# An S4 convolution block with a GEGLU: four early buffers, a small transfer scratch and a re-drawn order of tasks

## The chip, the cores and the metric

The kernel runs on one core of a Trainium2 chip. The core has a matrix engine (TensorE, PE in the profile), a vector engine (VectorE, DVE), an activation engine (ScalarE, ACT), GpSimd (POOL) and SyncE (SP). Each runs its own list of instructions in order, and they meet at semaphores. SP issues most transfers between memory and the on-chip SBUF. ACT and POOL issue a few of them. The metric is the device time of one launch in microseconds. Before the change it is 782.71 us, the median of three runs that lie between 780.6 and 785.24.

## The reference

One sequence of L = 2048 rows with D = 448 channels is taken through two halves of a block. Six rows of 448 numbers, made from the conditioning vector `c`, scale, shift and gate the halves.

```python
mod = (silu(c) @ w_mod).reshape(1, 6, 1, -1)
sa, ca, ga, sb, cb, gb = (mod[:, i] for i in range(6))
h = layernorm(x) * (1 + ca) + sa
x = x + ga * s4(h)
h = layernorm(x) * (1 + cb) + sb
x = x + gb * ((gelu(h @ w_gate) * (h @ w_up)) @ w_down)

def s4(u):
    dt = exp(log_dt)
    K = Re( sum_n C[d,n] * exp(dt * A[d,n] * l) * dt * B[d,n] )   # l = 0..L-1, 256 n per d
    return irfft(rfft(u, 2L) * rfft(K, 2L))[:L] + u * Dskip
```

The gate and up weights are 448 x 1792 each, the down weight is 1792 x 448. All inputs and the output are 32-bit floats.

## The kernel before, in words

**Tasks and their order.** The kernel doesn't call its engines where it describes the work. Each step is a task: `add(name, engine, ...)` records a name, an engine (or a choice of engines), a closure that emits the instructions, and the tasks it depends on. `Plan.order` then sorts all tasks by one number each and emits them in that order. The number comes from the table `PLACE`: for each name, a list of positions, one for each task of that name in the order of creation. A letter behind a number picks the engine where there is a choice (a for ACT, d for DVE, p for POOL, s for SP). Every engine executes its own tasks in that order. So the table sets which transfer stands ahead of which in a queue, and which copy stands ahead of which product on DVE. A wait on one task holds up everything behind it on the same engine.

**Three stages.** The work falls into three parts, and the table puts them one behind the other with overlaps.

1. *The filter and its spectrum.* The 448 channels are handled in subsets of 8, and these in three groups (the third one smaller). Four calls of `prep` load and prepare A, B, C and dt (`p.*`; the load `p.ld` at two loads a call), and `lt0`, `lt1` load prepared rows back. For each subset PE forms exponents and angles (`x.mm`, `y.mm`, `ang`, `anc`, lines 657 to 675). ACT takes exponentials (`x.exp`, `y.exp`, L644, L662), and sines and cosines (`sin`, `cos`, `sin2`, `cos2`, L680 to L699; `mag` at L683 strips a sign on DVE or ACT). DVE forms two products (`tx` at L721, `tyc` at L725). PE sums over n (`kgen`, L748). `kev` copies the sums out of PSUM. `kd`, `ka` and `kout` (L771 and after) do the first step of the transform of K, and leave it in `ako`. Beside this, the rows of x are loaded (`x.ld`, L852), normalized (`bn` at L877, `norm`) and taken through the first step of their own transform (`as`, `ua`, L984), which goes by memory (`ua.st` to u_d, `ub.u` back as ui, `ub.st` to us_d). The conditioning rows are made on the way (`m.ld`, `m.mm`). For groups 0 and 1, `k_fft` then works in batches. `f.fc` loads a piece of the constant matrices, and `f.ut` loads the spectrum of x. `f.fwd` (L1094) transforms K, `f.pr` (L1098) multiplies the spectra on DVE, `f.inv` (L1105) transforms back, `f.z` copies the result out of PSUM (by the helper at L482, ACT or DVE), and `f.st` (L1113) stores it to memory as y.
2. *The third group and the turn of the layout.* `ev_end` (task `ev.end`, L1051) closes the SBUF pools of the filter stage and opens those of the rest. `t_fft` does the spectra of the third group in nine pieces: `t.fwd`, `t.p0` and `t.p1` (products on DVE), `t.i0` with the copy `t.z0` and the store `t.s0` (L1224, to yb_d) for the rows that the first block of the output needs, and later `t.inv`, `t.z`, `t.st` (L1231) for the others. `yi.e` (L1288) loads what the first block needs of groups 0 and 1 (four transfers, all of them waiting for the stores of y), and `yi.l0`, `yi.l1` (L1297) load back from yb_d what the third group gives, piece by piece, by SP, ACT or POOL. `x1.ld` (L1265) loads the 512 rows of x of a block. The last step of the inverse transform for the first block is `co.mme` (L1404, channels of groups 0 and 1, 320 of them) and `co.mml` (L1409, the other 128). `co.adde` and `co.addl` (L1415, L1416) add x and take statistics on DVE. `co.rt` to `co.cb` normalize, scale and turn the result. The first weight tiles arrive by `w.le` (SP) and `w.la`, `w.ld` (all at L1332). Each is split in a high and a low half-precision part, `w.hi` (L1345, ACT) and `w.lo` (L1349 and L1350, DVE). A few idle matmuls (`spin`) and one idle square root on ACT (`warm`) stand where nothing else is to be done.
3. *The GEGLU.* There are four blocks of 512 rows. PE forms gate and up (`gu2`, `gu`, L1524, L1530), ACT the gelu (L1537), DVE the product (L1544). ACT and DVE split it again (L1556, L1559). PE does the down projection (L1599, L1630). The remaining `co.*` tasks of blocks 1 to 3 are worked in between, with `yi.ld` (L1278) and `x1.ld` for each.

**Where the early data lives.** Four loads of stage two have no input that depends on earlier work: the 896 KB of x rows for block 0 (`x1.ld` number 0), the first weight tile of 512 KB (`w.le` number 0), and two constants of 32 KB, `c.ai` (the matrix of `co.mm`) and `c.ih` (an identity in half precision, used by `spin` and the turns). In the kernel before, their buffers belong to pools that `ev_end` opens (`yp`, `ws`), so the four loads depend on `ev.end`. The weight loads depend on the x load `t_x` as well.

Of the kernel before, what the change touches and what calls it, by code (L numbers as in the profile page):

```python
# [11 lines left out]
FT = mybir.dt.float32  # L12
HF = mybir.dt.float16
# [10 lines left out]
L, D, N, FF = 2048, 448, 256, 1792  # L24
# [387 lines left out]
def s4_geglu(ctx: ExitStack, tc: tile.TileContext, a: dict, out: bass.AP):  # L412
    nc = tc.nc
# [1420 lines left out]
```

## Time and profile before

| | us |
|---|---|
| three runs | 780.6, 782.71, 785.24 |
| the profiled execution, its own time | 783.97 |
| its span | 782.0 |
| PE busy in the span | 728.2 |
| DVE busy | 590.7 |
| ACT busy | 459.6 |
| POOL busy | 8.4 |

The profile is one execution taken by the hardware profiler. Its mean granted TensorE clock is 0.993 of full speed. The span is the stretch from the first to the last instruction in the records, and 1.97 us of the device time lie outside it. A row of a group says: line, engine, operation, output <- inputs, shapes, count, then the busy time and the mean in ns of one, then the idle time of the engine just before these instructions, and what ended most of it. A row of a timeline says: start, length, engine, line, operation, output <- inputs, count, and in brackets the idle time just before and the event that ended it. Names with q behind an engine (SPq, DVEq) are the engine's own sequencer, which issues transfers. Engines overlap, so busy times don't add up to the span.

### The profile page before, as it was taken

How to read it: one execution, taken by the hardware profiler on the slowest of the kernel's cores; microseconds unless marked ns; L12 is line 12 of the kernel's file. 1: busy time of each engine (PE TensorE's matmuls, PEld its weight loads, DVE VectorE, ACT ScalarE, POOL GpSimd, SP SyncE). 2: the span in 40 equal slices, each digit the busy share in tenths (PEclk: the TensorE clock that was granted, in tenths of full speed). 3: DMA queues.
4: the chain of work that ended last, by engine and by line, in shares of the span. 5: the costliest groups of instructions: out<-in, count | busy, mean ns of one | idle time of the engine just before them, and what ended most of it. 6: DMA issues, size and time to landing. Idle time of an engine off the chain costs nothing.

```text
span 782.0 us, 19039 instructions
## 1 busy us (share of the span) xinstructions
PE 728.2 (93%) x8166; PEld 443.6 (57%) x8166; DVE 590.7 (76%) x889; ACT 459.6 (59%) x615; POOL 8.4 (1%) x23
## 2 busy tenths in 40 slices
PE   3677889998899999989999999999999999999998
PEld 1234444444577777677774445444694446944477
DVE  6999999999899999979767952569774587034743
ACT  5899998999899999862554730233411334022330
POOL 0000000000000000001200000000000000000000
PEclk9999999999999999999999999999999999999999
DMA  8645569998887598888876884355337224013201
GB/s 264 190 140 177 143 159 273 254 300 248 210 237 243 161 258 244 238 303 238 253 234 227 281 217 132 130 177 168 140 66 224 95 95 135 14 48 98 79 2 60
DMA packets 103950, 139.87 MB, mean 179 GB/s; under 512 B 34388, under 2 KB 85492, under 8 KB 103866
## 3 DMA queue, kind: packets, MB, share of 16 engines
q1 hardware_dynamic: 100436, 132.53, 57.8%
q10 hardware_dynamic: 2950, 5.38, 2.1%
q8 instruction: 64, 1.05, 0.6%
q0 software_dynamic: 480, 0.75, 0.3%
q14 instruction: 20, 0.16, 0.1%
HBM read 100.39 MB, written 36.01 MB: 174 GB/s over the span
## 4 chain that ended last, share of the span: by engine, by line
PE 66%; ACT 9%; DMA 8%; DVE 7%; issue 3%; SPq 2%; ACTq 0%; POOL 0%; DVEq 0%; POOLq 0%
PE pq L1530 24%; PE pq L1630 9%; PE pf L1105 5%; PE pg L675 4%; PE kg L748 4%; PE pd L1599 4%; PE pf L1094 3%; PE kg L771 2%; DMA w<-in_wgu 2%; PE pq L1524 2%; PE pd L1630 2%; ACT fg L688 1%; ACT my L662 1%; PE pf L984 1%; DVE ty L725 1%
## 5 line engine op out<-in xcount | busy, mean ns | idle before, releaser
L1530 PE MATMUL pq<-ht,wr 128*128 128x512 f16 (+1 forms) x1200 | 248.5, 365 | 0.4 <-DMA ht<-hl 0.4
L1530 PEld LDWEIGHTS <-wr 128*128 128x128 f16 x1200 | 114.5, 98 | 128.5 <-issue 11.8
L725 DVE TENSOR_TENSOR ty<-my,fg 128x2048 f32<-128x2048 f32 x56 | 127.6, 2281 | 0.0
L1537 ACT ACTIVATE ge<-pq 128x512 f32<-128x512 f32 (+1 forms) x60 | 33.8, 565 | 102.1 <-PE pq L1524 64.3
L1544 DVE TENSOR_TENSOR fq<-ge,pq 128x512 f32<-128x512 f32 (+1 forms) x60 | 38.9, 649 | 72.3 <-PE pq L1530 44.3
L1556 ACT ACTIVATE hh<-fq 128x1024 f16<-128x1024 f32 (+1 forms) x49 | 46.7, 961 | 65.0 <-DVE fq L1544 46.4
L721 DVE TENSOR_TENSOR tx<-mx,fg 128x1024 f32<-128x1024 f32 x56 | 67.8, 1216 | 4.4 <-ACT fg L692 3.0
L1630 PE MATMUL pq<-d,hh 128*128 128x224 f16 x476 | 68.9, 259 | 0.0
L748 PEld LDWEIGHTS kg<-ty,tx 128*32 128x32 f32 x3584 | 52.8, 110 | 21.6 <-issue 13.4
L748 PE MATMUL kg<-ty,tx 128*32 128x64 f32 x3584 | 61.5, 220 | 3.5 <-issue 1.6
L1559 DVE TENSOR_TENSOR hlo<-fq,hh 128x1024 f16<-128x1024 f32 (+1 forms) x49 | 53.7, 1106 | 13.4 <-ACT hh L1556 13.3
L1630 PE MATMUL pq<-d,hlo 128*128 128x224 f16 x238 | 61.7, 259 | 0.0
L688 ACT ACTIVATE fg<-pg 128x1024 f32<-128x1024 f32 x56 | 57.8, 1037 | 2.1 <-DVE tx L721 2.0
L662 ACT ACTIVATE my<-pg 128x1024 f32<-128x1024 f32 x56 | 55.5, 1033 | 3.7 <-PE pg L657 3.1
L1630 PEld LDWEIGHTS <-hh 128*128 128x128 f16 x560 | 54.2, 98 | 0.9 <-issue 0.2
L1105 PE MATMUL pf<-q,fc 128*128 128x160 f32 x264 | 43.4, 314 | 1.0 <-DVE q L1098 0.7
L1105 PEld LDWEIGHTS pf<-q,fc 128*128 128x128 f32 x264 | 37.5, 194 | 7.8 <-issue 4.7
L692 ACT ACTIVATE fg<-fg,small 128x1024 f32<-128x1024 f32 x36 | 41.4, 1170 | 0.1
L675 PEld LDWEIGHTS <-lt 64*128 64x128 bf16 x304 | 18.0, 94 | 37.1 <-issue 24.0
L675 PE MATMUL pg<-ea,lt 64*128 64x512 bf16 x152 | 31.4, 388 | 6.9 <-ACT fg L688 2.1
L1747 ACT ACTIVATE d<-fq 128x896 f16<-128x896 f32 x14 | 13.3, 947 | 39.8 <-PE pd L1599 27.3
L680 ACT ACTIVATE fg<-pg 128x1024 f32<-128x1024 f32 x30 | 31.1, 1037 | 2.0 <-PE pg L675 1.7
(208 smaller groups left out, 1121.8 us busy)
## 6 DMA issues: line engine op xcount, KB each, us to landing
wr<-w_d SPq DMA_DIRECT2D x21, 896.0 KB
fc<-in_k_fc SPq DMA_DIRECT2D x20, 576.0 KB
u_d<-so SPq DMA_DIRECT2D x32, 224.0 KB
ui<-u_d SPq DMA_DIRECT2D x10, 672.0 KB
fq<-in_wd SPq DMA_DIRECT2D x14, 448.0 KB
w<-in_wgu SPq DMA_DIRECT2D x11, 512.0 KB
us<-uo SPq DMA_DIRECT2D x22, 240.0 KB
q<-us SPq DMA_DIRECT2D x22, 240.0 KB
```

The source lines that it names most:

```text
L662: A.activation(yb.tile.rearrange("p h (n k) -> p n h k", n=2), pb.tile.rearrange("p (n h k) -> p n h k", n=2, h=2), AF.Exp)
L675: T.matmul(pa[:, nh * 512:nh * 512 + 512], w, x, start=(k == 0), stop=(k == 2))
L688: A.activation(fb.tile[:, 0].rearrange("p x (n k) -> p n x k", n=2), pb.tile.rearrange("p (n x k) -> p n x k", n=2, x=2), AF.Sin, scale=TW ...
L692: A.activation(fb.tile[:, 1], fb.tile[:, 1], AF.Sin, scale=-TWO_PI, bias=halfpi)
L721: V.tensor_mul(tx.tile, xb.tile[:, xm, None, :].to_broadcast([128, 2, 512]), fb.tile[:, :, 0])
L725: V.tensor_mul(ty.tile, yb.tile[:, :, None, :].to_broadcast([128, 2, 2, 512]), fb.tile[:, None, :, 1].to_broadcast([128, 2, 2, 512]))
L748: T.matmul(kg[32 * g:32 * g + 32, 2 * (s % 2) + q, :64], tx[:, r, nh, 4 * q + g], ty[:, 0:4:3, nh, 4 * q + g] if r else ty[:, 1:3, nh, 4 * ...
L1105: T.matmul(pz.tile[:, e % 32 - sl0], fc.tile[:, i, 1 + t], pp.tile[:, t, i], start=(t == 0 and e != 32), stop=(t == 1 and e != 0))
L1530: T.matmul(pb.tile[k][:, ts], wr.tile[:, 4 * lo + t, k, c0:c0 + 128], ht[:, m, ts], start=f % 2 == 0 and i == 0, stop=f % 2 == 1 and i == 9)
L1556: A.activation(hg.tile[0][:, cb, c], fq.tile[:, c], AF.Copy)
L1559: V.tensor_sub(hg.tile[1][:, cb, c], fq.tile[:, c], hg.tile[0][:, cb, c])
L1630: T.matmul(bank(k)[:, m], x[:, p, q[0], ts], w[:, p, q[1]], start=new and m == 0 and p == 0 and z == 0, skip_group_check=True, stop=i in ( ...
```

## The change

A new pool `ahead` is opened at the start of the kernel and stays to its end. It holds the two constants, the x rows of blocks 0 and 2, and the first weight tile. Those four loads lose their dependence on `ev.end` (and on `t_x`). The size of the scratch for dynamic transfers is given as 2048 bytes. Nothing else in the code differs but the table.

```diff
     keep = ctx.enter_context(tc.tile_pool(name="keep", bufs=1))
+    ahead = ctx.enter_context(tc.tile_pool(name="ahead", bufs=1, reuse_waits="tile"))
...
-        K2["ai"] = POOLS["yp"].tile([128, 64], FT, name="ai", bufs=1)
-        K2["ih"] = POOLS["yp"].tile([128, 128], HF, name="idenh", bufs=1)
...
-    K2 = {}
+    K2 = {"ai": ahead.tile([128, 64], FT, name="ai"), "ih": ahead.tile([128, 128], HF, name="idenh")}
...
-            xb.tile = POOLS["wk" if blk % 2 else "yp"].tile([128, 4, D], FT, name="x1", bufs=1)
+            xb.tile = (POOLS["wk"] if blk % 2 else ahead).tile([128, 4, D], FT, name="x1", bufs=1)
...
+        zero = cb + k == 0
...
-            wb.tile = POOLS["ws"].tile([128, 4, 256], FT, name="w")
+            wb.tile = (ahead if zero else POOLS["ws"]).tile([128, 4, 256], FT, name="w")
...
-            t1 = add("w.le", {"SP": 0.42}, -1350 + k + 2 * cb, ld, [EV["end"], t_x], [wb], kb=540)
+            t1 = add("w.le", {"SP": 0.42}, -1350 + k + 2 * cb, ld, [] if zero else [EV["end"], t_x], [wb], kb=540)
...
-    c_ai = sp("c.ai", 58, lambda: K2["ai"], lambda: a["k_ai"], 32, [EV["end"]])
-    c_ih = sp("c.ih", 58, lambda: K2["ih"], lambda: a["k_ih"], 32, [EV["end"]])
-    t_x = x1_load(0, [EV["end"]])
+    c_ai = sp("c.ai", 58, lambda: K2["ai"], lambda: a["k_ai"], 32)
+    c_ih = sp("c.ih", 58, lambda: K2["ih"], lambda: a["k_ih"], 32)
+    t_x = x1_load(0, [])
...
-    nc = _bacc.Bacc("TRN2", target_bir_lowering=False, num_devices=1)
+    nc = _bacc.Bacc("TRN2", target_bir_lowering=False, num_devices=1, dynamic_dma_scratch_size=2048)
```

In `PLACE` nearly every position below about 1480 is different, and nearly all from 1481 on are the same. The rows that the steps of this text touch, each with its positions before and after (long rows are cut behind the first entries):

```diff
-    "c.ai": "1250",
+    "c.ai": "133",
-    "c.ih": "1254",
+    "c.ih": "516",
-    "x1.ld": "1269 1463 1661 1782",
+    "x1.ld": "286 1463 1661 1782",
-    "w.le": "1304 1290 1351",
+    "w.le": "196 1300 1323",
-    "x.ld": "33 4 226 156",
+    "x.ld": "19 10 214 139",
-    "p.ld": "0 7 86 87 170 265 368 452",
+    "p.ld": "0 3 83 84 201 260 314 475",
-    "m.ld": "27 36 17 433 558 761",
+    "m.ld": "29 31 30 420 578 760",
-    "ub.u": "386 431 443 468 509 534 564 596 608 637 667",
+    "ub.u": "421 431 454 486 528 537 550 601 643 657 664",
-    "lt0": "61 112 302 369 561 744 852 1017",
+    "lt0": "64 144 325 368 560 801 861 985",
-    "lt1": "95 162 384 432 742 745 965 1060",
+    "lt1": "92 195 326 369 723 802 968 986",
-    "f.fc": "726 746 779 808
+    "f.fc": "724 731 767 790
-    "f.fwd": "727 759 786 809
+    "f.fwd": "746 759 787 820
-    "f.z": "755a 772d 812d 832a 865a 887d 908d 928a
+    "f.z": "757a 781a 809a 835a 869a 895d 912a 920a
-    "kev": "218d 224a 290d 317a 373d 394d 448a 490a
+    "kev": "199d 230d 290a 345a 378d 393a 462a 518d
-    "warm": "1263",
+    "warm": "1377",
-    "spin": "1353 1387 1388 1389 1392 1412",
+    "spin": "1394 1395 1396 1412 1413 1416",
-    "yi.l0": "1369s 1360s 1335p 1367p 1345s 1337p 1354p 1371p 1368p",
+    "yi.l0": "1309s 1344s 1342p 1315p 1353s 1347p 1351p 1357p 1359p",
-    "w.hi": "1341 1343 1356 1421 1460 1468 1487
+    "w.hi": "1267 1372 1363 1426 1455 1477 1487
```

312 rows, old and new, of the table PLACE are left out of this document.

## The prediction

> **What bounds the kernel now.** I read the windows view first, cut at the three points where the work changes its kind: the start, the last copy of the third group's K (349 us), the first gate/up matmul (387.4 us). Columns are span, then busy time and instructions of PE, PE weight loads, DVE, ACT, POOL, then clock, DMA share and GB/s.
>
> ```profile
> 0.00:349.00 349.00, 302.45 (x5294) 187.57 (x5294) 328.20 (x419) 318.66 (x403) 0.87 (x10) 0.99 0.78 224
> 349.00:387.40 38.40, 35.65 (x391) 29.88 (x392) 31.38 (x61) 14.91 (x32) 6.82 (x12) 1.00 0.81 245
> 387.40:782.00 394.60, 390.11 (x2484) 226.15 (x2482) 231.15 (x409) 125.98 (x182) 0.69 (x1) 1.00 0.44 133
> ```
>
> Stage one (0 to 349) belongs to DVE, with ACT 9.5 us behind it: DVE idles 20.8 us in all. Stage three belongs to PE: 390.11 of 394.60. Its time hardly depends on the order, and nearly all positions from 1481 on are the same in the new list. So a change of the total is a change of the moment at which stage three starts, now 387.4. Between them lies a short second stage, where a chain of small transfers decides. The chain of waits, in order of time:
>
> ```profile
> 360.03 4.92 DMA yb_d<-z
> ...
> 370.38 4.67 DMA yi<-yb_d
> ...
> 378.86 0.43 PE pd L1409 x4
> ...
> 387.45 2.29 PE pq L1530 x20
> ```
>
> Results of the last group go to memory (yb_d), come back turned (yi), and only then do the matmuls at L1409 (co.mml) run, at 378.86. Why the first yb_d store starts as late as 360.03 is seen on SP's queue. The first answer is of 340 to 360, the second of 356 to 360:
>
> ```profile
> 348.20 0.43 SPq L1265 DMA_DIRECT2D x<-in_A_u  x1
> 348.72 0.38 SPq L1113 DMA_DIRECT2D y<-zo  x1
> 349.20 10.73 SPq L1288 DMA_DIRECT2D yi<-y  x4
> 360.03 0.54 SPq L1224 DMA_DIRECT2D yb_d<-z  x1
> ```
>
> ```profile
> 358.71 1.22 SPq L1288 DMA_DIRECT2D yi<-y  x2
> ```
>
> The last two yi<-y issues wait for the y<-zo store of 348.72, and that store was issued right behind the 896 KB of x rows (348.20). SP stands until 358.71, and the yb_d stores stand behind it. POOL, which fetches most of yi back, waits for those stores and then has a backlog of seven issues:
>
> ```profile
> 369.29 3.81 POOL L1297 DMA_DIRECT2D yi<-yb_d  x7 [2.94 <-DMA yb_d<-z]
> ```
>
> **The change part by part.** The profiled run took 783.97 us: a span of 782.0 and 1.97 around it. It is 1.26 above the median of the runs shown, 782.71. The terms below are differences, so I apply them to the median as well.
>
> *The early buffers (x1.ld 1269 to 286, w.le[0] 1304 to 196, c.ai 1250 to 133, c.ih 1254 to 516).* No work is added. SP issues the same four transfers, of 896, 512, 32 and 32 KB. At the old place x rows leave the queue ahead of the y store: 0.918 MB at the 245 GB/s of 349 to 387 is 3.7 us. So SP should come free near 355 to 357 rather than 358.7 to 360, about when the first results (z0) exist. What then ends last in stage two is DVE. Its rows:
>
> ```profile
> 368.23 0.49 DVE L1415 TENSOR_TENSOR x<-x,pd 128x320 f32<-128x320 f32 x1
> 368.75 0.49 DVE L1416 BATCH_NORM_STATS2 st<-x 128x6 f32<-128x320 f32 x1
> ...
> 370.65 0.96 DVE L1349 SCALAR_TENSOR_TENSOR wr<-w,wr 128x768 f16<-128x768 f32 x1 [0.49 <-ACT wr L1345]
> 371.62 0.42 DVE L1350 SCALAR_TENSOR_TENSOR wr<-w,wr 64x256 f16<-64x256 f32 x1
> ...
> 377.05 0.96 DVE L1349 SCALAR_TENSOR_TENSOR wr<-w,wr 128x768 f16<-128x768 f32 x1 [1.87 <-ACT wr L1345]
> ...
> 379.33 0.29 DVE L1415 TENSOR_TENSOR x<-x,pd 128x128 f32<-128x128 f32 x1 [0.88 <-PE pd L1409]
> ```
>
> The spectral products end at 368.2; their number and place are the same in the new list. From there to the first addl (L1415 on 128 columns, 379.33) DVE has four adde of about 1.0 (0.49 and 0.49) and three w.lo of 1.4 (0.96 and 0.42). The new list adds one z0 copy, which waits for its matmuls, and one t.z copy. I estimate 0.9 and 0.7 for the two from the rows around them, which all last 0.4 to 1.0. Sum: 368.2 + 4.0 + 4.2 + 1.6 = 378.0, against 379.33, with no wait left in it: -1.3. The waits it replaces are the 1.87 and the 0.88, so the gain lies between 0 and 2.75. At worst the yb_d round trip still ends at 378.86 and nothing is gained. The new order also sends yi loads of finished pieces earlier on POOL (1315 against 1335) and lets the warm-up square-root table load go into ACT's wait (1377). I take **-1.6** for the stage, near the DVE sum and inside 0 to -2.75.
>
> *The new order in stage one: the start.* First tx on DVE waits for ACT:
>
> ```profile
> 42.30 1.23 DVE L721 TENSOR_TENSOR tx<-mx,fg 128x1024 f32<-128x1024 f32 x1 [0.95 <-ACT fg L699]
> ```
>
> Four sine passes stand ahead of it now, three in the new list (cos2 of the second subset goes behind), one pass of about 1.0 less. **-0.95**, between 0 (the wait comes elsewhere) and -0.95. Loads are re-sorted, but the five large ones ahead of the first K work stay the same bytes.
>
> *The first FFT batch.* PE waits for the filter constants, then DVE waits for PE:
>
> ```profile
> 199.00 1.46 PE L1094 MATMUL pf<-ako,fc 128*128 128x160 f32 x6 [1.86 <-DMA fc<-in_k_fc]
> ```
>
> ```profile
> 204.23 1.22 DVE L683 TENSOR_SCALAR fg<-pg 128x1024 int32<-128x1024 int32 x1 [2.36 <-PE pg L675]
> ```
>
> Today f.fc[0] stands at 726 and f.fwd[0] directly behind at 727, and six loads of lt follow in the same queue (742 to 745). In the new list the load is at 724 and its matmuls at 746, with six PE tasks between; two of the three lt pairs come later (801, 802), the third stands one place ahead of it. Bounds 0 and -2.36; I take half, **-1.2**, as one lt load is still in front.
>
> *Moves between ACT and DVE.* The list counts: f.z five fewer on DVE, kev two more, mag one more, ub.ev, p.e0, p.c0 (two) and so on. The two large prices:
>
> ```profile
> L683 DVE TENSOR_SCALAR fg<-pg 128x1024 int32<-128x1024 int32 x6 | 7.3, 1218 | 2.5 <-PE pg L675 2.4
> ...
> L482 DVE COPY zo<-pf 128x480 f32<-128x480 f32 x10 | 6.5, 649 | 0.2
> ...
> L482 DVE COPY ke<-kg 128x252 f32<-128x252 f32 x14 | 5.7, 410 | 0.8 <-PE kg L748 0.7
> ```
>
> -5 x 0.649 + 2 x 0.41 + 1.218 = -1.2 on DVE, and about -0.8 for the small ones: -2.0, and about as much more on ACT, which has 9.5 us more idle time but is as full in the middle. Between 0 and -2.0; I take half, **-1.0**.
>
> *What may cost.* In the new list m.ld[3] (784 KB) stands ahead of ub.u[0], whose matmuls follow three places later; today it stands behind. At 195 GB/s (row below) that is 0 to +4.1; SP can issue it while it still waits for the u_d stores, so I take 0. The early x and w loads run under stage one; 0 is taken, and their bound is the second rival. ACT's functions follow one another in the new list with as many changes of table as today: 0.
>
> *Sum:* -1.6 - 0.95 - 1.2 - 1.0 = -4.75. From the profiled run 779.2; from the median **778.0**.
>
> *Small scratch (2048 bytes).* Rows of POOL's transfers, by tile and by issue (KB each, us to landing):
>
> ```profile
> L1297 POOL DMA_DIRECT2D yi<-yb_d x10: 543/547/702, 365.7 to 374.2; - x10
> ```
>
> ```profile
> yi<-yb_d POOLq DMA_DIRECT2D x9, 32.0 KB, 4.5
> ```
>
> An issue takes 0.55 us, a landing 4.5: POOL does not wait for one to land before it issues the next. I take 0; the upper end is the third rival. The Trainium skill, "SBUF — State Buffer" (section "SBUF size: 192, 224, or 256?"), says that this scratch, 16 KiB by default, holds the ring of descriptors that POOL writes for its transfers. The Trainium skill, "DMA: Bandwidth & Descriptors" (section "Terms"), gives 16 bytes to a descriptor, by which, as an estimate, 2048 bytes hold 128 for each engine; no run here shows the limit. The Trainium skill, "SBUF — State Buffer" (section "SBUF: two separate sides"), speaks against the change's many POOL issues under a busy DVE: it has such a transfer take about 3.1 us instead of 0.62, and ten of them would add 25 us. By that rule the time would be that of the third rival; the trace does not agree, since the issues at 365.7 and after took 0.55 to 0.70 beside a DVE that worked without a gap.
>
> **The rivals.**
>
> 1. *Given back.* SP's gain is real but stage one finds new waits of the size of the old ones. Rows for: every wait named above is under 3 us and hangs on the order, and one that no order explains stays:
>
> ```profile
> 333.17 1.23 DVE L721 TENSOR_TENSOR tx<-mx,fg 128x1024 f32<-128x1024 f32 x1 [2.51 <-ACT fg L692]
> ```
>
> Two waits like this (2 x 2.4) cancel the sum: 782.71, say 780.5 to 784.5.
>
> 2. *The early loads collide (slower).* The w load (512 KB) and p.ld[4] (448 KB) are placed ahead of x.ld[2]. Today:
>
> ```profile
> 64.92 0.35 SPq L852 DMA_DIRECT2D xt<-in_A_u  x1
> ```
>
> ```profile
> 70.49 0.62 DVE L877 BATCH_NORM_STATS2 st<-xt 128x6 f32<-128x448 f32 x1
> ```
>
> ```profile
> 60.00:70.00 10.00, 7.05 (x112) 3.25 (x101) 9.76 (x13) 9.94 (x13) 0.00 (x0) 1.00 0.64 195
> ```
>
> From issue to first use are 5.57 us, of which 0.918 MB at 195 GB/s take 4.7: 0.9 of slack. 0.98 MB ahead cost 5.0, so DVE, which works in order, would stand 4.1 at the statistics with all its tx and ty behind them. The x rows (4.7 more) stand ahead of the puts of prep(1) and of lt0[2]. Sum +8.8: 786.8. It decides if the w load is still under way when x.ld[2] is issued. Against: the DMA share there is 0.64, and the w load waits for nothing, so SP can issue it early.
>
> 3. *POOL becomes serial* (ring too small, or the port rule): ten loads at 4.5 to landing, from about 364 (365.7 today, less the 1.6), end at 409 instead of 378.86: +30, 813.
>
> 4. *All waits go:* -2.75 - 0.95 - 2.36 - 2.0 - 2.51 = -10.6: 772.1.
>
> **How the numbers follow.** Forecast (775.5 to 780.5) 0.42; rival 1 0.23; rival 2 0.19; rival 3 0.03; rival 4 0.13. About 0.5% (3.9 us) is what a measurement of this kernel can tell from no change: below 778.8 is faster, above 786.6 slower. Faster: two thirds of the forecast (0.27) and rival 4: 0.40. Same: the rest (0.15) and rival 1: 0.38. Slower: rivals 2 and 3: 0.22. The range goes from rival 4's 772 to just above rival 2's 786.8, leaving out rival 3 and the worse half of rival 2.
>
> **What would show it.** Right: no x<-in_A_u on SP near 348; the second yi<-y pair under 356; first addl near 378; the first L1530 near 382 to 384 when the terms of stage one are in it. The fc wait at the first L1094 is short. Wrong: DVE waits before L877 near 70 us, or PE before the first L984 (rival 2); POOL issues of L1297 over 1 us or in steps of 4 (rival 3); a stage three longer than 394.6, which would mean that the order of the weights, not the start, has become the limit.

## The result, and the profile after

The changed kernel takes 777.02 us, the median of seven runs between 775.92 and 779.93. The kernel before takes 782.71 (780.6 to 785.24, seven runs). The ratio is 0.9916, with a 95% interval from 0.9888 to 0.9943, so the change is faster by 0.84%. This ratio and those below are the ones on record with their intervals. They aren't the quotients of the medians shown, which would be 0.9927 here. The prediction was 778.0, in a range from 772.0 to 787.5. The profiled execution of the changed kernel took 776.06 us with a span of 774.3. The two profiled executions are 7.91 us apart and the medians 5.69, so about 2 us of what the two traces show belongs to these two executions alone.

The windows view of both kernels, cut at two points that can be found in any order: the start of the last tx on DVE, and the first gate matmul at L1530. Before:

```profile
0.00:344.38 344.38, 298.85 (x5195) 184.55 (x5196) 325.33 (x413) 318.36 (x402) 0.87 (x10) 0.99 0.78 223
344.38:387.45 43.07, 39.30 (x492) 32.95 (x491) 34.25 (x68) 15.27 (x32) 6.82 (x12) 1.00 0.82 250
387.45:782.00 394.55, 390.06 (x2483) 226.10 (x2482) 231.15 (x409) 125.93 (x182) 0.69 (x1) 1.00 0.44 133
```

After:

```profile
0.00:339.54 339.54, 295.74 (x5197) 183.73 (x5198) 324.99 (x411) 319.19 (x403) 0.88 (x10) 0.99 0.80 230
339.54:380.80 41.26, 38.86 (x489) 32.64 (x489) 34.78 (x72) 15.77 (x34) 7.58 (x13) 1.00 0.74 219
380.80:774.30 393.50, 389.57 (x2482) 226.10 (x2481) 231.58 (x411) 124.69 (x177) 0.00 (x0) 1.00 0.44 134
```

Stage one is 4.84 shorter. DVE's busy time there falls by only 0.34 (325.33 to 324.99), and its idle time falls by 4.5 (19.05 to 14.55). Stage two is 1.81 shorter, and stage three 1.05. Where not said otherwise, the stages of any kernel below are cut at these two points.

In the timeline of SP no x rows stand near the end of stage one any more. The last y store goes out at 345.12, and the four yi<-y issues behind it end at 351.0. The first yb_d store follows when its data exists, at 351.94 instead of 360.03:

```profile
345.12 0.38 SPq L1112 DMA_DIRECT2D y<-zo  x1
345.60 5.40 SPq L1287 DMA_DIRECT2D yi<-y  x4
351.05 0.58 SPq L1139 DMA_DIRECT2D my<-in_k_ft  x1
351.94 1.76 SPq L1223 DMA_DIRECT2D yb_d<-z  x3
```

Transfers no longer end last in stage two. The timeline of DVE from the end of the spectral products to the first addl:

```profile
364.01 0.49 DVE L1415 TENSOR_TENSOR x<-x,pd 128x320 f32<-128x320 f32 x1
...
367.69 0.67 DVE L483 COPY lh<-pf 96x512 f32<-96x512 f32 x1
...
372.96 0.29 DVE L1415 TENSOR_TENSOR x<-x,pd 128x128 f32<-128x128 f32 x1 [0.52 <-PE pd L1409]
```

Between the first adde (364.01) and the first addl (372.96) DVE waits only for the 0.52 at the end. Before, the same stretch was 11.10 (368.23 to 379.33), with waits of 0.49, 1.87 and 0.88. The 0.52 is a wait for PE, and the chain of waits shows what PE did until then:

```profile
363.62 0.69 PE pq L1404 x4
...
365.39 7.16 PE pf L1206 x64
372.55 0.59 PE pd L1409 x8
```

From 365.39 PE works without a gap through later inverse transforms of the third group (L1206), which stand ahead of co.mml (L1409) in its list. So PE ends last here, with DVE 0.52 ahead of it. Before, the chain went by the transfers of yb_d, yi and y up to 378.86.

Two of the places that stage one's terms were taken from, after the change (timelines of DVE and PE):

```profile
41.20 1.23 DVE L722 TENSOR_TENSOR tx<-mx,fg 128x1024 f32<-128x1024 f32 x1
```

```profile
200.46 1.08 PE L1093 MATMUL pf<-ako,fc 128*128 128x160 f32 x6 [0.71 <-DMA fc<-in_k_fc]
```

The first tx no longer waits (0.95 before). PE's wait for the first filter constants is 0.71 instead of 1.86. The early loads are issued at 55.09 (weights) and 82.17 (x rows), and the statistics of the third x load don't wait:

```profile
67.35 0.62 DVE L878 BATCH_NORM_STATS2 st<-xt 128x6 f32<-128x448 f32 x1
```

POOL's issues of yi loads, by tile:

```profile
L1296 POOL DMA_DIRECT2D yi<-yb_d x10: 544/550/704, 357.1 to 367.0; - x10
```

They last 0.55 as before (0.547), under the scratch of 2048 bytes.

### The profile page after: what moved, and what is told of

Read it like the earlier page. It is cut to its first block, busy times and chain, and to the rows that moved or that the text cites. A ratio compares the mean times of both kernels' runs of the same rounds, so it can differ in the third digit from the quotient of the medians.

```text
span 774.3 us, 19010 instructions
## 1 busy us (share of the span) xinstructions
PE 724.2 (94%) x8166; PEld 442.5 (57%) x8166; DVE 591.3 (76%) x891; ACT 459.7 (59%) x613; POOL 8.5 (1%) x23
## 3 DMA queue, kind: packets, MB, share of 16 engines
q8 instruction: 64, 1.05, 0.6%
## 4 chain that ended last, share of the span: by engine, by line
PE 73%; ACT 12%; DVE 8%; DMA 4%; issue 2%; SPq 1%; DVEq 0%; ACTq 0%
PE pq L1530 32%; PE pq L1630 9%; PE pd L1599 4%; PE pg L676 4%; PE pf L1104 4%; PE kg L749 3%; ACT my L663 3%; DVE ty L726 2%; PE pq L1524 2%; PE pf L985 2%; PE pf L1093 2%; PE kg L772 2%; PE pf L1206 2%; ACT fg L689 2%; DMA us<-uo 2%
## 5 line engine op out<-in xcount | busy, mean ns | idle before, releaser
L1530 PE MATMUL pq<-ht,wr 128*128 128x512 f16 (+1 forms) x1200 | 248.3, 365 | 0.1
L1530 PEld LDWEIGHTS <-wr 128*128 128x128 f16 x1200 | 114.6, 98 | 128.5 <-issue 11.3
L689 ACT ACTIVATE fg<-pg 128x1024 f32<-128x1024 f32 x56 | 57.6, 1040 | 0.5 <-PE pg L676 0.3
L1104 PE MATMUL pf<-q,fc 128*128 128x160 f32 x264 | 41.5, 307 | 0.0
L985 PE MATMUL pf<-ui,fu 128*128 128x448 f32 x66 | 31.2, 576 | 1.2 <-DVE uo L993 0.5
```

The costliest lines, as they stand in the source:

```text
L689: A.activation(fb.tile[:, 0].rearrange("p x (n k) -> p n x k", n=2), pb.tile.rearrange("p (n x k) -> p n x k", n=2, x=2), AF.Sin, scale=TW ...
L985: T.matmul(pb.tile, fu.tile[:, i], ui.tile[:, EORD[e0 + i] % 32 - s0], start=True, stop=True)
L1104: T.matmul(pz.tile[:, e % 32 - sl0], fc.tile[:, i, 1 + t], pp.tile[:, t, i], start=(t == 0 and e != 32), stop=(t == 1 and e != 0))
L1530: T.matmul(pb.tile[k][:, ts], wr.tile[:, 4 * lo + t, k, c0:c0 + 128], ht[:, m, ts], start=f % 2 == 0 and i == 0, stop=f % 2 == 1 and i == 9)
```

## The experiments

The theory to be tested: the gain is made in two places, in stage one by the new order, and in stage two because SP is no longer held up behind the x rows. The main rivals were that one of the two makes all of it, and that the early loads cost stage one something. Each kernel was timed against the kernel before on the same chip, the flips kernel 6 times, one 11 times, the others 12 times. The medians of before in the three sets are 783.35, 783.31 and 783.32. The change has a set of its own (782.71 before, seven runs of each). Ratios are to the kernel before of the same set, and kernels of different sets are compared by them.

| kernel | median us | ratio | 95% interval |
|---|---|---|---|
| the change | 777.02 | 0.9916 | 0.9888 to 0.9943 |
| old order, early buffers | 786.04 | 1.0029 | 1.0005 to 1.0053 |
| new order, old buffers | 786.58 | 1.0039 | 1.0018 to 1.0059 |
| early buffers, new then old | 779.05 | 0.9935 | 0.9917 to 0.9954 |
| early buffers, old then new | 784.24 | 1.0007 | 0.9987 to 1.0027 |
| old order, early buffers, x rows at 1000 | 779.67 | 0.9943 | 0.9917 to 0.9969 |
| early buffers, new to 300, then old | 789.79 | 1.0066 | 1.0040 to 1.0092 |
| early buffers, new to 700, then old | 787.25 | 1.0042 | 1.0017 to 1.0066 |
| old order and buffers, new engine choices | 806.40 | 1.0295 | 1.0255 to 1.0334 |
| the change, x rows at 1000 | 778.86 | 0.9944 | 0.9920 to 0.9969 |
| the change, x rows late | 782.87 | 0.9997 | 0.9973 to 1.0021 |
| the change, first weights late | 779.67 | 0.9966 | 0.9945 to 0.9988 |
| before with the small scratch | 783.45 | 0.9995 | 0.9972 to 1.0017 |

### Buffers alone, order alone

Old order with the early buffers and the small scratch (`bufs_only`), against the kernel before:

```diff
-    "c.ai": "1250",
+    "c.ai": "133",
-    "c.ih": "1254",
+    "c.ih": "516",
-    "w.le": "1304 1290 1351",
+    "w.le": "196 1290 1351",
-    "x1.ld": "1269 1463 1661 1782",
+    "x1.ld": "286 1463 1661 1782",
...
+    ahead = ctx.enter_context(tc.tile_pool(name="ahead", bufs=1, reuse_waits="tile"))
```

> The old order with the four early buffers and the small scratch; only x1.ld (286), w.le[0] (196), c.ai (133) and c.ih (516) take the places of the new list. Theory (gain in two places: stage one by order, stage two because SP no longer stands behind the x rows): stage one as before, first yb_d store between 355 and 358 instead of 360.0, first addl about 1.3 to 1.6 earlier, 781.1 us. Rival (the order does it all, DVE ends last in stage two anyway): 782.7. Rival (early loads collide with x.ld[2]): a DVE wait ahead of the statistics near 70 us and 786 or more.

786.04 us: slower than before. Stage two did what the theory said, and stage one took it back and more. The windows view of this kernel:

```profile
0.00:349.84 349.84, 301.63 (x5198) 186.97 (x5198) 325.64 (x413) 319.45 (x402) 0.87 (x10) 0.97 0.79 224
349.84:391.43 41.59, 38.53 (x487) 32.50 (x487) 34.28 (x68) 15.32 (x32) 6.84 (x12) 1.00 0.78 222
```

Stage two is 41.59 (43.07 before). Stage one is 349.84 (344.38 before). So the second rival of the prediction comes true here in its size, but not at the place it named. Nothing waits at the statistics near 70 us. The x rows are issued between four u_d stores, and the stores' source buffers (so) come free late. The timelines of SP, ACT and DVE:

```profile
81.50 1.09 SPq L941 DMA_DIRECT2D u_d<-so  x2
82.65 0.57 SPq L1264 DMA_DIRECT2D x<-in_A_u  x1
83.77 1.58 SPq L941 DMA_DIRECT2D u_d<-so  x2
```

```profile
90.62 0.54 ACT L481 ACTIVATE so<-pf 128x448 f32<-128x448 f32 x1 [1.35 <-DMA u_d<-so]
```

```profile
98.66 0.69 DVE L539 TENSOR_TENSOR lh<-q,lh 112x512 bf16<-112x512 f32 x1 [2.81 <-ACT lh L481]
```

ACT waits 1.35 for a store to leave its buffer, its later tasks slide, and DVE waits 2.81 for one of them. These two waits don't add up to the 5.46 that stage one loses. Other waits of DVE are longer as well (3.2 for pg at L684, which was 2.4, and 2.1 at the first tx, which was 0.95), and the granted clock of the stage is 0.97 against 0.99. In the new order the four u_d stores go out together at 79.69, and the x rows behind them at 82.17.

New order with the old buffers (`order_only`; the small scratch stays), against the changed kernel:

```diff
-    "c.ai": "133",
+    "c.ai": "1250",
-    "c.ih": "516",
+    "c.ih": "1254",
-    "w.hi": "1267 1372
+    "w.hi": "1341 1372
-    "w.le": "196 1300 1323",
+    "w.le": "1304 1300 1323",
-    "x1.ld": "286 1463 1661 1782",
+    "x1.ld": "1270 1463 1661 1782",
...
-    ahead = ctx.enter_context(tc.tile_pool(name="ahead", bufs=1, reuse_waits="tile"))
```

> The new order with the four loads in the old buffers: x1.ld, w.le[0], c.ai, c.ih behind ev.end again (x rows directly ahead of the last y store, 1270), and the first w.hi at 1341 since its weights come late. Theory: stage one keeps its gain (last tx about 4.8 us earlier than in the profile of before), stage two gives nothing or loses 1 to 2 as SP stands behind the x rows again: 778 to 779.5 us. Rival (the order does it all): 777.0.

786.58 us: slower than before too, and above both expectations. Its trace keeps stage one (last tx at 339.45), and SP is held up by the x rows again, in the timeline of SP:

```profile
344.53 0.45 SPq L1265 DMA_DIRECT2D x<-in_A_u  x1
345.02 0.45 SPq L1140 DMA_DIRECT2D my<-in_k_ft  x1
345.57 0.38 SPq L1113 DMA_DIRECT2D y<-zo  x1
345.99 7.54 SPq L1288 DMA_DIRECT2D yi<-y  x4
```

The yi<-y issues last 7.54 instead of 5.40. Stage two as a whole is 47.54, which is 6.28 longer than in the changed kernel, at a granted clock of 0.96. The windows view, and the middle of the chain of waits:

```profile
339.45:386.99 47.54, 40.85 (x490) 34.15 (x490) 34.95 (x72) 15.65 (x34) 7.56 (x13) 0.96 0.79 233
```

```profile
363.44 3.51 DMA w<-in_wgu
366.98 4.83 DMA y<-lh
371.82 0.65 SPq L1297
```

SP's hold is 2.14 of the 6.28. Behind it the chain goes by the late weights: ACT waits 4.18 for them at 366.97, and a y store and the yi loads stand behind that. The profiled execution is the fastest of the twelve (782.23 against a median of 786.58), so the trace shows only part of the loss. Either half of the change alone, at the positions that the change gives it, makes the kernel slower. The effect is not a sum of the two.

### New order ahead of the seam, or behind it

In these kernels two tables stand in the code, and tasks under a position CUT of the first table go first, in its order and with its choice of engines. All others follow by the second table.

```diff
-        at = PLACE[n][i]
-        self.at, e = int(at.rstrip("adps")), at[-1]
+        at, late = FIRST[n][i], 0
+        if int(at.rstrip("adps")) >= CUT:
+            at, late = THEN[n][i], 10000
+        self.at, e = late + int(at.rstrip("adps")), at[-1]
```

With FIRST the new table, THEN the old one with early positions of the four loads, and CUT = 1250 (`new_then_old`):

> Early buffers; the tasks that stand ahead of ev.end in the new list come first in its order, all others follow in the old order. Theory: stage one's gain whole (last tx at 339.5), stage two as in the old order with SP free of the x rows: 777.5 to 778.5 us. Rival (the gain of stage one is lost where the old tail waits for transfers): 780 or more.

779.05 us, 0.55 above the expected span. The last tx starts at 341.49, not at 339.5. With FIRST the old table with the four early positions, THEN the new one, and CUT = 1248 (`old_then_new`):

> Early buffers; the tasks up to ev.end in the old order, all others in the new. Theory: last tx at 344.4 as before, stage two 1.8 and stage three up to 1.0 shorter: 780 to 781 us. Rival (all of the gain is made in stage one): 782.7. Rival (all of it behind stage one): 777.

784.24 us, above every expectation. Its stage one collides as in `bufs_only` (ACT waits 2.72 for u_d<-so, DVE 5.12 for lh), which the expectation had left out. Compared with what differs from them only behind the seam, both say the same of the new tail: `old_then_new` against `bufs_only` is 1.0007 against 1.0029, and the change against `new_then_old` is 0.9916 against 0.9935. That is 0.2% each, or 1.5 to 1.7 us, but in each pair the intervals overlap, so this gain isn't shown clear of the noise.

CUT = 300 and CUT = 700, with FIRST the new table:

> Early buffers; the tasks with positions under 300 in the new list first, in its order (start, first two prepared quarters, the w and x loads), all others in the old order. Theory (the start gives 0.95, the new neighbourhood at 60 to 100 us keeps the early loads from colliding): last tx near 343.4, stage two 41.6: 779.5 to 781 us. Rival (the whole order is needed, the old remainder meets new waits behind the cut): 784 or more. Rival (all of stage one's gain is made here): 777.5.

> As new_to_300 with the cut at 700, ahead of the first FFT batches. Theory (stage one's gain is spread: 0.95 at the start, 0.5 to 1.5 here, the mag wait of 2.4 and the last tx wait of 2.5 behind it): 778.5 to 780.5 us. Rival (the gain is all behind 700): as new_to_300.

789.79 us, as the rival had it (784 or more), and 787.25 us, closer to the first kernel than to its own theory. Cut inside stage one, the new order is slower than the old. With the cut at 300 new waits appear. The timelines of ACT and DVE of that kernel:

```profile
98.86 1.02 ACT L915 ACTIVATE fg<-pg 128x1024 f32<-128x1024 f32 x1 [4.51 <-PE pg L902]
```

```profile
103.98 0.29 DVE L1138 TENSOR_SCALAR as<-au,rs 128x128 f32<-128x128 f32 x1 [4.15 <-PE pf L1148]
```

Stage one's gain can't be traced to a stretch of the order in this way: each seam brings waits of its own.

### The x rows at another early place

The old order with early buffers, one transfer moved (`bufs_x1000`, against `bufs_only`):

```diff
-    "x1.ld": "286 1463 1661 1782",
+    "x1.ld": "1000 1463 1661 1782",
```

> As bufs_only, but the x rows (x1.ld number 0) at position 1000 of the old order instead of 286, so that they are loaded far from the u_d stores near 83 us. Theory (in the old order the 896 KB stand between the u_d stores, the so buffers come free late, ACT and then DVE wait 1.35 and 2.81 us at 90 to 99, and this is most of what bufs_only lost): no such wait, stage one within 1.5 us of the profile of before, stage two 41.4 to 41.6: 781 to 782.5 us. Rival (any early load costs stage one its 4 to 5 us, by traffic or by the clock that is granted): 785 to 787.

779.67 us, below what was expected. One load of 896 KB moved out from between the u_d stores is worth 0.86% (1.0029 to 0.9943), and the intervals are clear of each other. The four u_d stores now go out together at 81.97, the ACT wait is gone, the DVE wait on lh is 0.29, and stage one is 343.14 instead of 349.84. So the place of this one load made the loss of `bufs_only`. That it went by the so buffers alone isn't shown: the two waits that went are 1.35 and 2.52 us, and the kernel gained 6.4. This version keeps the old order everywhere else and has two thirds of the change's gain (0.57% of 0.84%). The same move in the changed kernel (`after_x1000`):

> The changed kernel with one transfer moved: x1.ld number 0 at position 1000 instead of 286. In the old order the same move took bufs_only from 786.0 to 779.7. Theory (the new order keeps the u_d stores near 82 us clear of the x rows, and no wait on them shows in its trace, so there is nothing to gain): 776.5 to 778 us. Rival (the x rows at 286 cost something in the new order too, by traffic): 773 to 775.5, faster than the changed kernel.

778.86 us, a ratio of 0.9944 against 0.9916, with intervals that overlap: nothing gained. That fits the theory, although the median lies 0.86 above the expected span. No version ran faster than the change.

### What the late loads cost in the new order

One load of the changed kernel late, with its buffer early: the x rows at 1270 (`x_late`), or the first weights at 1304 with their w.hi at 1341 (`w_late`).

```diff
-    "x1.ld": "286 1463 1661 1782",
+    "x1.ld": "1270 1463 1661 1782",
```

> The changed kernel with x1.ld number 0 at 1270, behind ev.end and ahead of the last y store, as in the kernel before; its buffer stays early, and the weight and the constants are loaded early. Prediction's step (x rows hold up SP at the yi<-y issues, 1.6 lost at the transition): 778 to 779.5 us. Rival (from the trace of order_only: SP comes free at 353.5 instead of 351.0, but the DVE products end at 363.1 either way, so the x rows' place costs nothing here): 776.5 to 777.5.

782.87 us, slower than either expectation: the late x rows alone take back the whole gain (0.9997). The profiled execution doesn't show it. It took 776.15, and the other eleven took 781.24 to 786.1. In its trace SP's yi<-y issues last 7.21 and stage two 42.25, 0.99 more than in the changed kernel:

```profile
338.65:380.90 42.25, 39.18 (x489) 32.70 (x489) 34.83 (x72) 15.66 (x34) 7.57 (x13) 1.00 0.80 237
```

Where the other eleven lose some 5 us more stays open, since no trace of them exists.

> The changed kernel with the first weight load at 1304 and its w.hi at 1341, as in order_only, but x rows and constants early. Theory (order_only lost its 9.6 us against the changed kernel because ACT waits for weights, 4.2 and 2.9 us at 367 and 371 in its trace, and stores y and issues yi loads behind that): 781 to 785 us. Rival (x rows and weights together are needed, each alone costs under 1.5): 777 to 778.5.

779.67 us, between the two expectations. The late weights cost 0.5% (0.9966 against 0.9916). Its trace has a stage two of 42.46, and ACT waits 0.43 for the weights there, not the 4.18 of `order_only`; a second wait of 2.96 is put down to a yi load. By the ratios the late x rows cost 0.81% and the late weights 0.50%, together 1.31%, near the 1.23% that `order_only` lost. So the larger part of that loss is the x rows. In the one trace of `order_only`, its fastest execution, the chain goes by the weights instead. Of the slower ones there is no trace.

### The engine choices, and the scratch

The kernel before with the new choice between ACT and DVE for the 54 tasks ahead of ev.end that differ (`flips_only`). Some of the entries:

```diff
-    "mag": "518a 587a 610a 597d 670a 680d
+    "mag": "518a 587a 610a 597d 670d 680a
...
-    "p.c0": "26a 159d 428d 632d",
+    "p.c0": "26a 159d 428a 632a",
```

> The kernel before with its buffers and order; only the choice between ACT and DVE of the 54 tasks ahead of ev.end that differ is taken from the new list. Prediction's step: -1.0, between 0 and -2.0: 782.4 us where before is 783.35. By the two traces (DVE busy ahead of the last tx 325.33 and 324.99): -0.3 at most. Rival (flips fit only the new order, as they put work into waits that are elsewhere in the old one): +1 to +3.

806.4 us, far outside every expectation. The windows view up to the first product of the third group (350.60 before, 371.65 here), of before and of this kernel:

```profile
0.00:350.60 350.60, 303.71 (x5305) 188.83 (x5306) 328.21 (x420) 320.24 (x404) 0.87 (x10) 0.99 0.78 224
```

```profile
0.00:371.65 371.65, 308.92 (x5305) 191.40 (x5306) 327.12 (x416) 324.06 (x408) 0.87 (x10) 0.97 0.73 211
```

DVE's busy time falls by 1.09, as large as the step of the prediction. Its idle time rises from 22.39 to 44.53. Its waits that end on ACT, added up in the waits view of these stretches, rise from 6.3 to 21.6: most of the idle time that is new comes from waiting for ACT. The granted clock is lower too, and PE's busy time is 5.21 longer.

The kernel before with the small scratch and nothing else (`scratch_only`):

```diff
-    nc = _bacc.Bacc("TRN2", target_bir_lowering=False, num_devices=1)
+    nc = _bacc.Bacc("TRN2", target_bir_lowering=False, num_devices=1, dynamic_dma_scratch_size=2048)
```

> The kernel before with the small scratch and nothing else, so the same instructions. Theory (the scratch costs and gains nothing; POOL's issues of L1297 last 0.54 to 0.70): 783.3 us within 1; its profile is a second look at the order before, where the wait of 2.51 ahead of the tx near 333 should come again if it belongs to the order, and not if it belongs to that execution. Rival (POOL waits for room in a small ring): issues over 1 us and 790 or more.

783.45 us: no difference. Since it has the same instructions, its trace is a second look at the kernel before. Three rows of DVE's timeline stand against the rows that the prediction's terms came from:

```profile
41.88 1.22 DVE L721 TENSOR_TENSOR tx<-mx,fg 128x1024 f32<-128x1024 f32 x1 [0.53 <-ACT fg L699]
```

```profile
202.30 1.23 DVE L683 TENSOR_SCALAR fg<-pg 128x1024 int32<-128x1024 int32 x1 [1.10 <-PE pg L675]
```

```profile
330.12 1.23 DVE L721 TENSOR_TENSOR tx<-mx,fg 128x1024 f32<-128x1024 f32 x1 [0.37 <-ACT fg L692]
```

The waits of 0.95, 2.36 and 2.51 are 0.53, 1.10 and 0.37 here. Its last tx starts at 341.33, which is 3.05 earlier than in the first trace of the same order. Stage two is 43.96, and SP's four yi<-y issues last 8.42 instead of 10.73, though the x rows stand ahead of them here too.

## Why the prediction was right

The total was right (778.0 against 777.02), and so for the most part was the reading that the gain comes from an earlier start of stage three: of the 7.70 between the two spans, 6.65 are that earlier start. It came at 380.80, ahead of the 382 to 384 that the prediction gave as a sign, since this pair of traces lies further apart than the medians. The terms were not all of the right size, and their errors cancelled. That the total is so close is in part luck.

**The early buffers (forecast -1.6).** That they shorten stage two was right. In the old order stage two is 41.59 and 41.62 with early buffers (`bufs_only`, `bufs_x1000`) and 43.07 and 43.96 with late ones (the kernel before, `scratch_only`): 1.45 to 2.37 shorter. The path was only half right. As forecast, the round trip of transfers no longer ends last. But then it is PE that does, 0.52 behind DVE, and not DVE. The first addl came 8.95 behind the first adde, where the forecast's own list (the adde, the w.lo, and the copies) gave 9.8. SP's hold was overrated, too. The 10.73 belong to one execution. The second look at the same instructions has 8.42, and early x rows in the old order (`bufs_x1000`) have 7.94. In the new order it is 5.40 with early x rows, and 7.21 and 7.54 with late ones. So the x rows' part of the hold is between 0.5 and 2.8. The rest of it stays with early x rows as well. By timing, the early buffers in the old order, with the x rows kept away from the u_d stores, gain 0.57% (3.6 us by the medians), and late x rows in the new order cost 0.8%. Of this, the traces place 1.0 to 2.4 in stage two. The rest isn't located.

**The start, the first FFT batch, the engine moves (forecast -0.95, -1.2, -1.0, together -3.15).** Two traces gave -4.84 for stage one. As evidence this is weak, because the same old order took 344.38 in one execution and 341.33 in another. Three traces of the old order without the collision have a stage one of 341.33 to 344.38, with a mean of 342.95, and six of the new order 338.65 to 342.91, with a mean of 340.44. The means are 2.5 apart, but the two ranges overlap. By timing, what the new order of stage one adds over the old one without the collision is the difference of `new_then_old` (0.9935) and `bufs_x1000` (0.9943): 0.6 us, with intervals that overlap. The step that failed is pricing a term at a wait that was seen in one execution. The start held best: in those three traces of the old order the first tx waits 0.53 to 1.17, and in none of the six of the new order. The wait for the filter constants is no property of the order: 0.64 to 1.86 in the old one, and from none to 1.61 in the new one. The wait of 2.36, which bounded that term, was 1.10 in the second look. The engine moves gave -0.34 of DVE time in the change, and on their own cost 23 us. In `flips_only` DVE's busy time fell by 1.09, about the half that was taken of the summed -2.0, and busy time was the wrong thing to sum. How much of the -3.15 stage one's order really gives is between nothing and some 3 us, and the runs don't settle it.

**Stage three (forecast 0).** The pair of traces has it 1.05 shorter. With the new tail it was 393.4 to 393.5 in every trace. With the old tail it was between 393.4 and 396.9, and early buffers don't decide it (393.44 in `bufs_x1000`, 394.72 in `new_then_old`). With the old tail PE waits for the first turned rows in most traces (0.4 for ht<-hl before, 0.7 in `scratch_only`, 1.1 in `new_then_old`, none in `bufs_x1000`), and with the new tail it doesn't wait there in any. The two pairs of kernels put the whole new tail, stage two included, at 1.5 to 1.7, with intervals that overlap. The prediction had put nothing here, which makes up for part of what stage one didn't give.

**The scratch (forecast 0).** Right: 0.9995, and issues of 0.55. The prediction weighed them against a rule of the Trainium skill, "SBUF — State Buffer" (section "SBUF: two separate sides"), and said that the trace does not agree. That went too far. The page's case of 3.1 us is a transfer beside a DVE copy, in a mode that takes the port DVE shares with POOL. Beside the ten issues, before and after, DVE forms products (L1196, L1199) and sums (L1415, lines as after) of a tile in SBUF with one in PSUM, takes statistics, splits weights and copies from PSUM. No copy from SBUF to SBUF is among them, so no run here shows the page's case. Nor was DVE without a gap there before: it idles 0.49 ahead of 370.65.

**Rival 1, given back:** not seen. The new waits of DVE in stage one are small, the longest 0.74 at the first L1097. Behind the last tx there are 1.23 on ke and 2.64 ahead of the first product of the third group, which waited 2.08 before as well. **Rival 2, the early loads collide:** false for the change, true in its outcome for the old order, where it turned a gain of 0.57% into a loss of 0.29%. In the trace it sits at the buffers of the u_d stores, not at the x load that the prediction named. In the new order the stores go ahead of the load. **Rival 3, POOL serial:** false. **Rival 4, all waits go:** the 2.51 was gone, but it is gone from the second trace of the old order as well, so it can't be counted as a gain of the change.

## What to carry to other kernels

Loading early was worth it here, where the late transfer stands ahead of a store that many wait for, but the new place must be checked for stores whose buffers are about to be reused. One load at one of two early places made 0.86% of difference. A wait of one or two microseconds in one profiled execution is not yet a property of the program: look at a second execution of the same instructions before it becomes a term of a sum. An order drawn as a whole couldn't be priced by its parts here: each part alone, at the positions of the new list (buffers, order, engine choices, the first 300 or 700 positions), made the kernel slower, and the buffers alone gained once a single load was moved.

## What the runs showed of the hardware that was not expected

The same program spreads by more than the change is worth: 34 of 35 executions of the kernel before lie between 778.66 and 789.35 us. The granted clock goes with it. The nine of them with a clock of 0.995 or more have a median of 780.85, and the six with 0.989 or less one of 785.28. The other two sets of the same kernel show it too (781.75 against 784.23, and 782.00 against 786.12). Which of the two is the cause isn't shown. Kernels differ in it as well: the median clock of the runs is 0.984 in `flips_only`, 0.989 to 0.990 in `bufs_only`, `order_only`, `old_then_new` and `new_to_300`, 0.992 to 0.993 in the kernel before, and 0.995 in the change. So part of what separates these kernels may be the clock, and no run tells it apart from the waits.

With late x rows the profiled execution took 776.15 at a clock of 0.997, and the eleven others 781.24 to 786.1 at 0.988 to 0.998. One of these ran at 0.998 and took 783.07, so the clock alone doesn't explain that gap.
